# Linear attention and mixture of experts on one core: q and k loaded as whole runs, SyncE's queue in the order of the steps

## The chip, the cores and the metric

One core of a Trainium2 chip runs the whole program. The metric is the time of one execution on the device in microseconds. Engines are named as in the profile: PE is TensorE, PEld its weight loads, DVE is VectorE, ACT is ScalarE, POOL is GpSimd, SP is SyncE, whose queue issues nearly all transfers here (SPq in the rows).

## What is computed

Two parts follow each other. The first is attention with a feature map, on 8 batches of 8 heads with 576 tokens of 64 values; the second sends each token of the result (4608 rows of 512) through one of 8 experts, if its skip score is above 0.

```python
def phi(x):
    proj = np.einsum('bhsd,df->bhsf', x, w_phi)
    proj = proj - np.max(np.abs(proj), axis=-1, keepdims=True)
    return np.concatenate([np.exp(proj), np.exp(-proj)], axis=-1)
q_p, k_p = (phi(q), phi(k))
kv = np.einsum('bhsf,bhsd->bhfd', k_p, v)
z = np.sum(k_p, axis=2)
num = np.einsum('bhsf,bhfd->bhsd', q_p, kv)
den = np.einsum('bhsf,bhf->bhs', q_p, z)[..., None] + 1e-06
...
out = x.copy()
...
y[mask] = gate_w[mask, None] * (np.maximum(xc[mask] @ w1[e], 0.0) @ w2[e])
out[do_compute] = xc + y
```

## The kernel before

**Units and steps.** The attention works in units of four heads: 16 units of k and 16 of q, since a batch has two of each. A unit has five items. Item 0 is the tail, the last 2 tokens of each run of 18; items 1 to 4 are the other 16 tokens, in four parts. A head is 32 runs of 18 tokens, and a run is contiguous in memory. The program walks through steps: in step t, item t of the k stream and item t - 6 of the q stream enter, and each later stage takes the item that entered some steps earlier (projection 1, exponential 3, sums 4, use 5, and 6 for the table of a unit). So unit n of k enters in steps 5n to 5n+4, unit n of q in steps 5n+6 to 5n+10.

**A unit's way.** `st_load` (line 251) brings the unit into the tile `raw`. Its partitions are (half of d, head of the pair, run), and it holds 2 pairs of heads x 18 tokens x 32 values; one transfer per pair and half of d, so four per unit, in pieces of 32 values (128 bytes), because half of a token's 64 values lie together. `st_t` (line 276) transposes it on VectorE in 32 x 32 blocks: the tail at item 0 (line 289, tile `xTt`), and 512 columns each at items 1 and 3 (line 291, `xT`). ScalarE writes the rounded part `hi` (line 292), GpSimd or VectorE the rest `lo` (line 294), and TensorE projects both (lines 306 to 308). VectorE then takes the largest absolute value of each row (line 312) and subtracts it (line 321, tile `u`). For k, the exponentials are multiplied with `v` (lines 388 and 395); for q, with the table that comes of that (lines 465 and 486), and `norm` (lines 433 to 450) divides.

**Loads and stores.** `raw` has four buffers, `hi` and `lo` five each (pool `hl`). `f_t` asks for the next unit's load when a unit's item 0 enters, for either kind (line 720). `v` is asked for by `st_loadv` in step 5n+2 and its tails `vt` by `st_loadvt` in step 5n+3. Stores are put off by two steps (`store_half`, lines 503 and 505; `store_rows`, lines 564 and 566) and by seven (`rest`, lines 630 and 635); the stores of the attention's rows go to `xrows`, those of line 630 and 635 to the output.

**What sets the order.** Each engine runs its instructions in one fixed order, and SP its transfers too. A planner makes that order when the program is built: it takes what its own model says is ready, by the place in the program. TensorE is left out of that between steps 8 and 79, where its instructions stand in the program's order (`manual_schedule`, from line 724). SP's order is the planner's throughout. An instruction whose data has not come holds all behind it on its engine.

**The experts** follow: weights come in pieces of 512 KB (`load_chunk`, lines 184 and 187), ScalarE and VectorE or GpSimd split them into two parts (lines 188 and 189), TensorE multiplies, and rows are scattered to the output. Their tiles lie where the attention's were.

Of the kernel before, what the change touches and what calls it, by code (L numbers as in the profile page):

```python
# [8 lines left out]
F32 = mybir.dt.float32  # L9
# [9 lines left out]
P = 128  # L19
SLOT = 256  # L20
CFG = {'ql': -2, 'q1': 0, 'vtl': 3, 'at': 6, 'cp': 0, 'ini': 'vvpvppvvpvp', 'inz': '', 'lo': {('E', 0): 'pppvpppp', ('E', 1): 'pppppppp'}, 'lod': 'vppvvvpv', 'seq': ('E', 'E', 'C', 'C', 'SC', 'D', 'DS', 'C', 'C', 'D'), 'pre': (2,), 'rows': (1, 2), 'rxg': (0,) * 6, 'lag': (1, 3, 4, 5, 6), 'post': (4, 5, 7), 'hook': (-1, -1, -1), 'man': (8, 79), 'dnow': 0, 'off': 6, 'order': 'EPAZUT', 'direct': (), 'nb': {'K': 1, 'P': 3, 'U': 2, 'O': 2}, 'apools': (('ld', 2), ('hl', 5), ('up', 5), ('zp', 2), ('ep', 7), ('kvp', 6), ('xp', 2)), 'mpools': (('rawp', 1), ('mx', 2), ('mo', 2), ('wseta', 1), ('wsetb', 1))}
# [3 lines left out]
def kernel(  # L25
# [12 lines left out]
    nc = tc.nc  # L38
    B, H, S, D = q.shape
    NF = w_phi.shape[1]  # L40
    E = w_gate.shape[1]
# [9 lines left out]
    NAUG = D + E + 2  # L51
    NA1 = NAUG - 1
    # a row of xrows: the token, its gate, its number
# [3 lines left out]
    # slots: full ones, ones of up to 192 tokens, ones of up to 128  # L57
# [13 lines left out]
    xrows = dram.tile([NTOK, XW], F32, name="xrows")  # L71
# [35 lines left out]
    # the tails of a quad's v, each pair in its own rows, zeros in the other's  # L107
# [16 lines left out]
    # of every slot: the rows to gather and the rows to scatter to  # L124
# [85 lines left out]
    def places(g, pad, v):  # L210
        # v is 0 in an empty place, else 1 + the row to gather; what to add so that no row is scattered from an empty one
        nc.vector.tensor_scalar(out=g, in0=v, scalar1=-1.0, scalar2=0.0, op0=ALU.add, op1=ALU.max)
        nc.vector.tensor_scalar(out=pad, in0=v, scalar1=0.0, scalar2=BIG, op0=ALU.is_equal, op1=ALU.mult)

    early = []
    # ------------------------------------------------------------------ attention
    with ExitStack() as actx:
        pools = {}
        for nm, bufs in CFG["apools"]:
            pools[nm] = actx.enter_context(tc.tile_pool(name=nm, bufs=bufs))  # L220
        ld, hl, zp, up, ep, kvp, xp = (pools[nm] for nm in ("ld", "hl", "zp", "up", "ep", "kvp", "xp"))

        # a head is 32 runs of 18 tokens; partition (half of d, head of the pair, run)
        kv_in = {
            "k": k.rearrange("b h s d -> (b h s d)").rearrange("(u r p t c) -> u r p t c", r=2, p=64, t=18, c=D),
            "q": q.rearrange("b h s d -> (b h s d)").rearrange("(u r p t c) -> u r p t c", r=2, p=64, t=18, c=D),
        }
        vv = v.rearrange("b h s d -> (b h s d)").rearrange("(u h p t c) -> u p h t c", h=4, p=32, t=18, c=D)
        outv = out.rearrange("(b p j) m -> b p j m", p=32, j=18)
        # rows of xrows: two batches after each other, then the tails of both  # L230
# [20 lines left out]
        def st_load(u):  # L251
            src = kv_in[u.kind]
            u.raw = ld.tile([P, 2, 18, 32], F32, tag="raw", name="raw", bufs=4)
            for pr in range(2):
                for dh in range(2):
                    nc.sync.dma_start(
                        out=u.raw[dh * 64:dh * 64 + 64, pr],
                        in_=src[u.g, pr][:, :, dh * 32:dh * 32 + 32],
                    )
# [16 lines left out]
        def st_t(u, i):  # L276
            if i == 0:
                n, sfx = P, "t"
                src = u.raw[:, :, 16:18, :].rearrange("p r t c -> p r (t c)")
            elif i in (1, 3):  # L280
                n, sfx = 4 * P, ""
                src = u.raw[:, i // 2, 0:16, :].rearrange("p (q g) c -> p q g c", g=4)
            else:
                return
            xT = hl.tile([P, n], F32, tag="xT" + sfx, name="xT" + sfx, bufs=2)
            hi = hl.tile([P, n], F32R, tag="hi" + sfx, name="hi" + sfx)
            lo = hl.tile([P, n], F32R, tag="lo" + sfx, name="lo" + sfx)
            if i == 0:
                nc.vector.transpose(out=xT.rearrange("p (r c) -> p r c", r=2), in_=src)  # L289
            else:  # L290
                nc.vector.transpose(out=xT.rearrange("p (g q c) -> p q g c", g=4, q=4), in_=src)
            nc.scalar.activation(out=hi, in_=xT, func=AF.Copy)  # L292
# [140 lines left out]
        def norm(o, xdst, ldst, shape):  # L433
            # o: [P, 4, NAUG]
# [8 lines left out]
            a, c = shape  # L443
# [8 lines left out]
        def st_use_q(u, i):  # L452
# [5 lines left out]
            if i == 0:  # L458
                # the tails of two batches side by side
# [39 lines left out]
            if i == 4:  # L499
                c = slice(0, 4 * D)  # L500
# [12 lines left out]
        def post(b):  # L513
# [41 lines left out]
            # the gate goes with the token's row  # L555
# [21 lines left out]
            def rank():  # L577
                # rank of each computed token among those of its expert
# [133 lines left out]
        def f_t():  # L712
            for items, us, off in streams:
                s = now[0] - off
                if s == CFG["ql"]:
                    st_load(us[0])
                if 0 <= s < n:
                    u, i = items[s]
                    st_t(u, i)
                    if i == 0 and s // 5 + 1 < len(us):  # L720
                        st_load(us[s // 5 + 1])

        man = None
        for t in range(n + OFF + LA):
# [64 lines left out]
    def hidden_c(hv):  # L789
        # 192 tokens: the last 64 with both their parts next to each other  # L790
# [9 lines left out]
    def half1(ws, xs):  # L800
        # a slot of 128 tokens: the tokens' columns stay, the weights stream
# [53 lines left out]
    def mm1(ws, xs, hooks=()):  # L855
# [73 lines left out]
    # the slots of the tokens that are left: per expert full ones of 256, a rest of up to 192 or of up to 128 in  # L929
    # one of its own kind  # L930
# [5 lines left out]
    def tables():  # L936
# [24 lines left out]
        # a token's column: its rank, in groups of 128, plus cf[0] where it is below cf[1], else plus cf[2]  # L961
# [8 lines left out]
        # the experts of the slots, and how many there are  # L970
# [8 lines left out]
        # the column of each token  # L979
# [46 lines left out]
        # the slots that the sequence below leaves  # L1026
# [18 lines left out]
    # the slots in their order; a half one goes along with a full one  # L1045
# [50 lines left out]
    # whatever the slots above don't hold  # L1096
# [38 lines left out]
```

## Time and profile before

| | us |
|---|---|
| median of 3 runs | 684.47 |
| lowest and highest run | 684.28, 689.55 |
| span of the profiled execution, first to last instruction | 681.4 |
| attention runs evenly (stretch used below) | 20 to 350 |
| last attention work and tables of the experts | about 350 to 430 |
| experts | 430 to 681 |

The profile gives the span of one execution and no other time for it; the span is 3.1 us under the median of the runs. In its rows, a group is written as line, engine, operation, tile written <- tile read, shapes and count; then busy us, mean ns of one, and the idle time of the engine just before these instructions with what ended it. A timeline row starts with the start in us and the duration. A row of a stretch gives, for each engine, its busy time in it and the number of instructions.

### The profile page before, as it was taken

The numbers are of one execution on the slowest core, as the hardware profiler recorded it, in microseconds if no ns is written. First come the engines' busy times: TensorE is split into PE (matmuls) and PEld (weight loads), VectorE is DVE, ScalarE is ACT, GpSimd is POOL, SyncE is SP. The second block draws the span as 40 slices with busy tenths as digits, with TensorE's granted clock in tenths as the row PEclk, the third lists the DMA queues.
The fourth block names the chain that finished last, engine by engine and source line by source line (L and its number), as shares of the span: only waits on it lengthen the run. The fifth ranks groups of instructions, "written<-read, shape, count | busy, mean of one in ns | idle before, by whom it ended". The sixth has DMA issues, their size and how long they took to land. (4 is left out here: it accounts for less than half of the span.)

```text
span 681.4 us, 16258 instructions
## 1 busy us (share of the span) xinstructions
PE 600.5 (88%) x6045; PEld 514.2 (75%) x6045; DVE 539.6 (79%) x1216; ACT 373.7 (55%) x747; POOL 440.7 (65%) x383
## 2 busy tenths in 40 slices
PE   4897999979998889999899991999999989979994
PEld 3585888768877778877788881888878879868893
DVE  6868888887978978978998799679988876677830
ACT  4566665647565475656564533147757556555510
POOL 6886777777777596868774458276575485374411
PEclk9898999999999999999999996899989999999998
DMA  9898664857675667655316387269788877774500
GB/s 130 127 145 157 112 168 91 160 108 133 144 144 90 146 117 133 142 103 114 105 33 195 114 222 232 72 203 296 249 262 268 268 238 267 251 238 139 192 17 27
DMA packets 221684, 108.17 MB, mean 159 GB/s; under 512 B 160293, under 2 KB 202405, under 8 KB 221604
## 3 DMA queue, kind: packets, MB, share of 16 engines
q1 hardware_dynamic: 218272, 97.60, 58.8%
q0 software_dynamic: 3200, 9.45, 4.0%
q8 instruction: 49, 0.80, 0.5%
q14 instruction: 31, 0.25, 0.1%
q10 hardware_dynamic: 132, 0.07, 0.0%
HBM read 83.86 MB, written 24.02 MB: 158 GB/s over the span
## 5 line engine op out<-in xcount | busy, mean ns | idle before, releaser
L189 POOL TENSOR_TENSOR w<-wraw_c,w 128x1024 fp32r<-128x1024 f32 x45 | 109.9, 2454 | 70.6 <-ACT w L188 64.3
L188 ACT ACTIVATE w<-wraw_c 128x1024 fp32r<-128x1024 f32 x96 | 101.0, 1057 | 56.9 <-DMA wraw_c<-in_moe_w_dram 44.9
L353 POOL TENSOR_TENSOR z<-ek 128x512 f32<-128x512 f32 x64 | 81.7, 1277 | 54.9 <-ACT ek L345 45.1
L312 DVE TENSOR_REDUCE m<-ps_P 128x4 f32<-128x512 f32 (+1 forms) x160 | 96.4, 620 | 3.7 <-PE ps_P L308 3.6
L321 DVE TENSOR_TENSOR u<-ps_P,m 128x512 f32<-128x512 f32 (+1 forms) x160 | 95.9, 621 | 0.4
L306 PE MATMUL ps_P<-wph,hi 128*128 128x256 f32 x256 | 80.8, 316 | 16.6 <-ACT hi L292 8.5
L486 PEld LDWEIGHTS ps_O<-kva,eq 128*64 128x64 f32 x2048 | 75.2, 137 | 18.0 <-ACT eqt L373 7.3
L189 DVE TENSOR_TENSOR w<-wraw_c,w 128x1024 fp32r<-128x1024 f32 x51 | 75.4, 1481 | 14.6 <-ACT w L188 14.5
L486 PE MATMUL ps_O<-kva,eq 128*64 128x74 f32 x2048 | 78.4, 229 | 5.0 <-ACT eqt L373 3.2
L294 POOL TENSOR_TENSOR lo<-xT,hi 128x512 fp32r<-128x512 f32 x61 | 78.1, 1280 | 5.0 <-ACT hi L292 4.8
L308 PE MATMUL ps_P<-wph,lo 128*128 128x256 f32 x256 | 73.4, 287 | 0.0
L307 PE MATMUL ps_P<-wpl,hi 128*128 128x256 f32 x256 | 73.2, 286 | 0.0
L388 PE MATMUL ps_K<-ek,v 128*64 128x256 f32 x512 | 71.3, 396 | 1.5 <-DMA v<-in_v_dram 1.5
L372 ACT ACTIVATE eq<-ps_U 128x512 f32<-128x512 f32 x64 | 37.9, 593 | 57.2 <-PE ps_U L366 49.2
L306 PEld LDWEIGHTS ps_P<-wph,hi 128*128 128x128 f32 x256 | 49.4, 193 | 20.4 <-ACT hi L292 9.0
L908 PE MATMUL ps_O<-w,hh 128*128 128x512 f32 x160 | 62.4, 400 | 1.4 <-DVE hh L796 1.3
L836 POOL DMA_INDIRECT out_dram<-o,si x17 | 22.2, 1305 | 54.1 <-DVE o L834 44.4
L913 PE MATMUL ps_O<-w,hlo 128*128 128x512 f32 x120 | 49.0, 410 | 5.1 <-DVE hlo L796 5.1
L307 PEld LDWEIGHTS ps_P<-wpl,hi 128*128 128x128 f32 x256 | 49.7, 194 | 0.0
L308 PEld LDWEIGHTS ps_P<-wph,lo 128*128 128x128 f32 x256 | 49.6, 194 | 0.2 <-DVE lo L294 0.2
L366 PE MATMUL ps_U<-ident,u 128*128 128x128 f32 x288 | 48.4, 286 | 0.6 <-DVE u L321 0.6
L289 DVE STREAM_TRANSPOSE xTt<-raw 128x128 f32<-128x128 f32 x32 | 9.9, 309 | 48.8 <-DMA raw<-in_k_dram 26.8
(233 smaller groups left out, 1570.9 us busy)
## 6 DMA issues: line engine op xcount, KB each, us to landing
wraw_c<-in_moe_w_dram SPq DMA_DIRECT2D x96, 512.0 KB, 4.6
raw<-in_k_dram SPq DMA_DIRECT2D x64, 144.0 KB, 4.0
raw<-in_q_dram SPq DMA_DIRECT2D x64, 144.0 KB, 4.1
v<-in_v_dram SPq DMA_DIRECT2D x64, 128.0 KB, 3.7
out_dram<-xm SPq DMA_DIRECT2D x32, 256.0 KB, 4.4
xrows<-xm SPq DMA_DIRECT2D x8, 516.0 KB, 4.2
xrows<-xm SPq DMA_DIRECT2D x8, 512.0 KB, 4.7
vt<-in_v_dram SPq DMA_DIRECT2D x64, 16.0 KB, 2.6
```

The costliest lines, as they stand in the source:

```text
L188: nc.scalar.activation(out=hi, in_=raw, func=AF.Copy)
L189: (eng or nc.vector).tensor_tensor(out=lo, in0=raw, in1=hi.bitcast(F32), op=ALU.subtract)
L294: (nc.vector if CFG["ini"][nlo[0] - 1:nlo[0]] == "v" else nc.gpsimd).tensor_tensor(out=lo, in0=xT, in1=hi.bitcast(F32), op=ALU.subtract)
L306: nc.tensor.matmul(o, hi[:, c], wph, start=True, stop=False)
L307: nc.tensor.matmul(o, hi[:, c], wpl, start=False, stop=False)
L308: nc.tensor.matmul(o, lo[:, c], wph, start=False, stop=True)
L312: nc.vector.tensor_reduce(out=m[:, 0:nt], in_=pv, axis=AX.X, op=ALU.max, apply_absolute_value=True)
L321: nc.vector.tensor_tensor(out=uu[:, 0:nt, :], in0=pv, in1=m[:, 0:nt].rearrange("p (t o) -> p t o", o=1).broadcast_to([P, nt, NF]), op=ALU. ...
L353: zeng.tensor_tensor(out=z, in0=e[:, 0:2, :], in1=e[:, 2:4, :], op=ALU.add)
L388: nc.tensor.matmul(o[hd * 64:hd * 64 + 64, :], u.v[:, 2 * pr + hd, g * D:(g + 1) * D], u.e[i][:, 2 * j + hd, :], start=(g == 0), stop=False,)
L486: nc.tensor.matmul(ov[s * 64:s * 64 + 64, 2 * j + hd, :], e[:, half, j, hd, s * 64:s * 64 + 64], kva[:, half, 2 * pr + hd, :], start=(half ...
L908: nc.tensor.matmul(y[sub], hh[:, t], wh[:, fi, :], start=first, stop=False)
```

## The change

`raw` now holds all 64 values of each token: [128, 2, 18, 64], with three buffers. One transfer per half of d, so two per unit: each brings 64 partitions x 2 pairs, and for each the whole run of 18 tokens from the half's first value on, less the last 32 values, 1,120 values (4,480 bytes) in one piece. Both halves of d so arrive in either half of the partitions, and the transposes read the first 32 of every 64 values of a token. `hl` has four buffers for five. The next unit of q is asked for when item 3 of a q unit enters, and no longer item 0; for k it stays item 0. All that SP issues from the first step to the end of the attention is put in the program's order; the first unit's load stands before it and the experts' loads after it. Comments that the diff takes out are left out here.

```diff
-... ('hl', 5), ...
+... ('hl', 4), ...
...
-        kv_in = {
-            "k": k.rearrange("b h s d -> (b h s d)").rearrange("(u r p t c) -> u r p t c", r=2, p=64, t=18, c=D),
-            "q": q.rearrange("b h s d -> (b h s d)").rearrange("(u r p t c) -> u r p t c", r=2, p=64, t=18, c=D),
-        }
+        RUN = 18 * D
+        HD = D // 2
...
         def st_load(u):
-            src = kv_in[u.kind]
-            u.raw = ld.tile([P, 2, 18, 32], F32, tag="raw", name="raw", bufs=4)
-            for pr in range(2):
-                for dh in range(2):
-                    nc.sync.dma_start(
-                        out=u.raw[dh * 64:dh * 64 + 64, pr],
-                        in_=src[u.g, pr][:, :, dh * 32:dh * 32 + 32],
-                    )
+            x = q if u.kind == "q" else k
+            u.raw = ld.tile([P, 2, 18, D], F32, tag="raw", name="raw", bufs=3)
+            for r, run, n, dh in [(dh * 64, 0, 64, dh) for dh in range(2)]:
+                nc.sync.dma_start(
+                    out=u.raw[r:r + n].rearrange("p r t c -> p r (t c)")[:, :, 0:RUN - HD],
+                    in_=bass.AP(
+                        tensor=x.tensor, offset=x.offset + (u.g * 128 + run) * RUN + dh * HD,
+                        ap=[[RUN, n], [64 * RUN, 2], [1, RUN - HD]]))
...
-                src = u.raw[:, :, 16:18, :].rearrange("p r t c -> p r (t c)")
+                src = u.raw[:, :, 16:18, 0:HD]
...
-                src = u.raw[:, i // 2, 0:16, :].rearrange("p (q g) c -> p q g c", g=4)
+                src = u.raw[:, i // 2, 0:16, 0:HD].rearrange("p (q g) c -> p q g c", g=4)
...
-                nc.vector.transpose(out=xT.rearrange("p (r c) -> p r c", r=2), in_=src)
+                nc.vector.transpose(out=xT.rearrange("p (r t c) -> p r t c", r=2, t=2), in_=src)
...
-                    if i == 0 and s // 5 + 1 < len(us):
+                    if i == (0 if u.kind == "k" else 3) and s // 5 + 1 < len(us):
                         st_load(us[s // 5 + 1])
...
+        sman = actx.enter_context(ExitStack())
+        sman.enter_context(tc.manual_schedule(engines={mybir.EngineType.SP}))
         for t in range(n + OFF + LA):
...
             if t == 1:
                 setup()
+        sman.close()
```

More of the change, by code (lines that the diff above doesn't have):

```diff
@@ L20 @@
 SLOT = 256
-CFG = {'ql': -2, 'q1': 0, 'vtl': 3, 'at': 6, 'cp': 0, 'ini': 'vvpvppvvpvp', 'inz': '', 'lo': {('E', 0): 'pppvpppp', ('E', 1): 'pppppppp'}, 'lod': 'vppvvvpv', 'seq': ('E', 'E', 'C', 'C', 'SC', 'D', 'DS', 'C', 'C', 'D'), 'pre': (2,), 'rows': (1, 2), 'rxg': (0,) * 6, 'lag': (1, 3, 4, 5, 6), 'post': (4, 5, 7), 'hook': (-1, -1, -1), 'man': (8, 79), 'dnow': 0, 'off': 6, 'order': 'EPAZUT', 'direct': (), 'nb': {'K': 1, 'P': 3, 'U': 2, 'O': 2}, 'apools': (('ld', 2), ('hl', 5), ('up', 5), ('zp', 2), ('ep', 7), ('kvp', 6), ('xp', 2)), 'mpools': (('rawp', 1), ('mx', 2), ('mo', 2), ('wseta', 1), ('wsetb', 1))}
+CFG = {'ql': -2, 'q1': 0, 'vtl': 3, 'at': 6, 'cp': 0, 'ini': 'vvpvppvvpvp', 'inz': '', 'lo': {('E', 0): 'pppvpppp', ('E', 1): 'pppppppp'}, 'lod': 'vppvvvpv', 'seq': ('E', 'E', 'C', 'C', 'SC', 'D', 'DS', 'C', 'C', 'D'), 'pre': (2,), 'rows': (1, 2), 'rxg': (0,) * 6, 'lag': (1, 3, 4, 5, 6), 'post': (4, 5, 7), 'hook': (-1, -1, -1), 'man': (8, 79), 'dnow': 0, 'off': 6, 'order': 'EPAZUT', 'direct': (), 'nb': {'K': 1, 'P': 3, 'U': 2, 'O': 2}, 'apools': (('ld', 2), ('hl', 4), ('up', 5), ('zp', 2), ('ep', 7), ('kvp', 6), ('xp', 2)), 'mpools': (('rawp', 1), ('mx', 2), ('mo', 2), ('wseta', 1), ('wsetb', 1))}
 @with_exitstack
```

## The prediction

> **What bounds the kernel now.** I read the page's busy line first, then busy time by stretches, then who waits for whom, then single loads in the timeline.
>
> ```profile
> span 681.4 us, 16258 instructions
> PE 600.5 (88%) x6045; PEld 514.2 (75%) x6045; DVE 539.6 (79%) x1216; ACT 373.7 (55%) x747; POOL 440.7 (65%) x383
> ...
> 20.00:350.00 330.00, 301.17 (x3859) 251.48 (x3860) 275.74 (x765) 200.48 (x474) 251.64 (x240) 0.99 0.64 125
> ...
> L289 DVE STREAM_TRANSPOSE xTt<-raw 128x128 f32<-128x128 f32 x29 | 9.0, 310 | 48.2 <-DMA raw<-in_k_dram 26.2 <-DMA raw<-in_q_dram 18.2 <-POOL z L359 2.2
> L291 DVE STREAM_TRANSPOSE xT<-raw 128x512 f32<-128x512 f32 x59 | 41.2, 698 | 0.0
> L292 ACT ACTIVATE hi<-xT 128x512 fp32r<-128x512 f32 x58 | 36.4, 627 | 2.5 <-DVE xT L291 1.5 <-PE ps_P L307 0.6 <-DVE den L437 0.3
> ```
>
> The third line is the stretch in which the attention runs evenly. Columns: stretch, length, busy us of PE, PEld, DVE, ACT, POOL, then granted clock, DMA share, GB/s. By the whole span TensorE is the fullest engine. In this stretch VectorE is: 275.7 us busy and 48.2 us idle ahead of one instruction, the transpose of a unit's tail (line 289), make 323.9 of 330. TensorE leaves 330 - 301.2 = 28.8 us. So a microsecond more of waiting on `raw` costs about a microsecond, and one less gains at most until TensorE is full: 28.8 us in all. The 512-column transposes (line 291) never wait; the tail is the first reader of a unit and takes the whole wait.
>
> ```profile
> DVE xTt L289 <- DMA raw<-in_k_dram: 26.8, 14, 4.0
> DVE xTt L289 <- DMA raw<-in_q_dram: 18.2, 12, 3.4
> PE ps_P L306 <- DVE u L321: 12.3, 12, 3.8
> PE ps_O L486 <- ACT eqt L373: 3.2, 4, 1.1
> PE ps_O L486 <- DVE lgm L449: 1.4, 2, 0.8
> ACT w L188 <- DMA wraw_c<-in_moe_w_dram: 44.9, 39, 4.3
> ```
>
> Columns: us in total, times, longest. 45.0 us over 32 units is 1.41 us a unit. TensorE's answer to late VectorE work is 12.3 + 3.2 + 1.4 = 16.9 us.
>
> ```profile
> 163.04 3.10 SPq L256 DMA_DIRECT2D raw<-in_k_dram  x4
> 169.44 0.31 DVE L289 STREAM_TRANSPOSE xTt<-raw 128x128 f32<-128x128 f32 x1 [1.96 <-DMA raw<-in_k_dram]
> ...
> 289.26 2.21 SPq L256 DMA_DIRECT2D raw<-in_q_dram  x3
> 292.24 0.64 SPq L256 DMA_DIRECT2D raw<-in_q_dram  x1
> 298.10 0.31 DVE L289 STREAM_TRANSPOSE xTt<-raw 128x128 f32<-128x128 f32 x1 [3.44 <-DMA raw<-in_q_dram]
> 300.57 0.36 PE L306 MATMUL ps_P<-wph,hit 128*128 128x256 f32 x1 [1.47 <-DVE u L321]
> ```
>
> Two loads. The k load is first issued at 163.04; VectorE comes to its tail 4.44 us later (169.44 - 1.96 - 163.04) and the data 6.40 us later. The q load: 5.40 and 8.84. VectorE's order was fixed by the planner, which put the tail some 4.4 to 5.4 us of other work behind the load; the load takes 6.4 us or more. The wait is thus not late data as such, it is a tail queued too soon, and VectorE's other work stands behind it. The last row is TensorE paying 1.47 us of the 3.44.
>
> **The change part by part.**
>
> ```profile
> wraw_c<-in_moe_w_dram SPq DMA_DIRECT2D x96, 512.0 KB, 4.6
> raw<-in_k_dram SPq DMA_DIRECT2D x64, 144.0 KB, 4.0
> raw<-in_q_dram SPq DMA_DIRECT2D x64, 144.0 KB, 4.1
> v<-in_v_dram SPq DMA_DIRECT2D x64, 128.0 KB, 3.7
> ...
> 118.50:121.00 2.50, 2.50 (x33) 1.93 (x34) 2.43 (x8) 2.13 (x5) 0.74 (x1) 1.00 0.98 155
> 240.00:242.00 2.00, 1.67 (x22) 1.67 (x22) 0.60 (x4) 1.53 (x5) 2.00 (x3) 1.00 1.09 223
> 505.00:508.00 3.00, 3.00 (x25) 2.73 (x24) 3.00 (x5) 1.93 (x3) 1.73 (x1) 1.00 0.85 270
> ```
>
> The loads. A unit was 4 x 147,456 = 589,824 bytes in 128-byte pieces; the stretch at 118.5, where one such load runs, moved 155 GB/s with the DMA engines full (0.98): 589,824 / 155 = 3.8 us. Now each of two loads brings 64 partitions x 2 runs x 4,480 bytes = 573,440 bytes, both halves of d in either half of the partitions: 1,146,880 bytes a unit. The nearest rates for long pieces: v into 32 partitions, 223 GB/s at a full share (240 to 242), and weights into 128 partitions, 270 at 0.85, so 318 at a full one. That is 5.1 us or 3.6 us a unit. I take 223: a share of 1.09 says the engines were held up at that rate with 1-KB pieces, which a narrow destination explains, and 64 partitions are also not the whole width. The other end stays in the range.
>
> The Trainium skill, "SBUF — State Buffer", section "Door 1: The DMA port swizzle (why [64,N] ≈ [32,N])", says that partitions 0 to 63 reach only half of the DMA ports, so that 64 partitions get no more bandwidth than 32, and under "Can I just issue two DMAs to hit both halves?" that two such transfers serialize. By that rule the unit costs the 5.1 us and the sum below stands; without it 3.6 us, and the sum would be that of the third rival. The trace agrees as far as the 223 GB/s go; no run here yet shows 64 partitions with long runs.
>
> Time to land. v lands 3.7 us after issue, of which 131,072 bytes / 223 = 0.6 move: 3.1 us are fixed. A unit then lands 3.1 + 5.1 = 8.2 us after its first issue (3.1 + 3.6 = 6.7 at the fast rate), against 6.4 and 8.84 in the two rows above; four issues took 3.10 us of SP, two will take about half, which is inside the 8.2.
>
> Where VectorE stands then. Nothing shows where the planner will put the tails. Two ends: the distance stays at about 5 us, and the wait is 8.2 - 5 = 3.2 us, 1.8 more than 1.41, x 32 = +58 us; or the planner moves every tail behind its landing, and all 45.0 us go, of which TensorE lets 28.8 through. Between them I go by the row nearest in kind, the 96 weight loads of 512 KB in long pieces: ScalarE waits 44.9 / 96 = 0.47 us for one, so the planner's idea of such a load is short by that much at the fast rate. Two loads of that size at the slow rate are 5.1 - 3.6 = 1.5 us longer than at the fast one: 0.47 + 1.5 = 1.97 us a unit, 0.56 more than now, x 32 = +18 us. With VectorE full this is time of the kernel.
>
> Contention. 1.3 us more of transfer for each of the 29 units in 330 us brings the share from 0.64 to 0.64 + 38/330 = 0.75. DMA does not become the bound; loads that meet stores come later, which the upper end holds.
>
> ```profile
> SPq L503 <- DVE lgm L449: 15.1, 2, 9.3
> SPq L630 <- DVE lgm L449: 14.0, 3, 6.0
> SPq L564 <- DVE xt L561: 10.6, 3, 4.2
> SPq L635 <- DVE lgt L449: 8.3, 4, 3.5
> ```
>
> SyncE in the order of the steps. In a period of five steps SP now issues: k's next load (step 5n), the stores that fell due, v (5n+2), vt (5n+3), q's next load (moved from the q unit's item 0 to its item 3, step 5n+4). A store that waits for VectorE's norm holds v, vt and both loads behind it; these waits are already 15.1 + 14.0 + 10.6 + 8.3 = 48.0 us, in an order in which loads could pass. By the program q's load stands two steps ahead of its tail and k's five. The stretch holds 29 units, so a step is 330 / 29 / 2.5 = 4.6 us: 9.1 us for q against 8.2 to land, 23 for k. TensorE's need is met; what a held store costs appears as the tail's wait on VectorE. Price 0 to +48; I take 0, since the waits for q now (18.2), with v and vt partly ahead of it, are no larger than those for k (26.8).
>
> Three unit buffers. q n takes the buffer of k n, which is free at step 5n+3, one step before the load; k n+1 takes that of q n-2, free at 5n-1. No wait is added as long as VectorE keeps the program's order; price 0.
>
> `hl` from 5 to 4. ScalarE's write of `hi` waits for TensorE 0.6 us in all with five (the line 292 row above). With four a tile is asked for again five steps later and read for three; price 0 to a few times 0.6, I take 0.
>
> The strided transposes read 32 elements in 64. No row shows such a read; a penalty would lengthen the 698 ns, a gain isn't excluded by a row but has no cause. Taken as 0, the upper end in the range. One semaphore wait less or two per tail: nothing that I count.
>
> ```profile
> 7.11 0.71 DVE L291 STREAM_TRANSPOSE xT<-raw 128x512 f32<-128x512 f32 x1 [1.93 <-DMA raw<-in_k_dram]
> ...
> 0.79 8.87 SPq L256 DMA_DIRECT2D raw<-in_k_dram  x8
> ```
>
> The start. Now the first transpose needs the first two loads of four; then it needs both. 0.79 + 8.2 = 9.0 against 7.11: +2 us.
>
> ```profile
> 366.12 0.92 SPq L184 DMA_DIRECT2D wraw_c<-in_moe_w_dram  x1
> ...
> 397.37 0.57 SPq L566 DMA_DIRECT2D xrows<-xt  x1
> ```
>
> The end. The first expert weights are loaded at 366 among the attention's stores. They lie outside the ordered part, so they may still pass; were they held until the last store, 31 us later, TensorE would come to them cold. Price 0, else some of these 31.
>
> Sum: 18 + 2 = +20 on the profiled span of 681.4, so 701.4. The profile gives no time of its own beside its span; the runs' median of 684.47 is 3.1 above it, and I put the 3.1 around the new span too: 704.5.
>
> **The rivals.**
> 1. Faster: the tails fall behind their landings. Place: line 289. It decides where VectorE comes to the tail more than 8.2 - 1.41 = 6.8 us after the load's first issue. For it: k's load is asked for five steps ahead. Against it: the 4.44 and 5.40, tails pulled forward as soon as the planner thinks they can. TensorE's 16.9 us go, and the start costs 2: 684.5 - 15 = 669.5. If all its idle time went, 657.7.
> 2. No change: the planner counts the added bytes in full, and tail and landing move together. The start alone: 686.5.
> 3. The longer pieces pay in full: the loads run at the fast rate, land after 6.7 us and wait 0.47 us a unit. (1.41 - 0.47) x 32 = 30 us less, cut to the 16.9: 669.5 again.
> 4. Slower still: SP held by its stores. All 48 us shown: 704.5 + 48 = 752; half of it: 728.
>
> **How the numbers follow.** Forecast (704.5, its own range 692 to 730) and rival 4 together 0.45, of which rival 4 is 0.07; rival 2 0.18; rivals 1 and 3 0.29 and 0.08. A measurement of this kernel tells about 1% (6.8 us) from no change. Faster is 0.37, same 0.18, slower 0.45. Both signs hold much, so the range goes from 665 (most of the faster cases) to 728.
>
> **What would show it.** Right: line 289's idle time on `raw` above 48 us; two SP issues and 8 us to landing; a DMA share near 0.75 in the same stretch; 223 GB/s where a unit loads alone. Wrong: the share falls below 0.64 or the rate passes 300 GB/s (rate); the wait falls below 20 us and TensorE's share of the stretch rises above 0.95 (placing); SP idle on line 503 or 630 with a `raw` issue behind it (order).

## The result, and the profile after

The changed kernel takes 765.66 us (median of 4 runs, 761.41 to 766.63), the kernel before 684.38 us beside it (4 runs, 682.85 to 689.55). The ratio is 1.1146 with a 95% interval of 1.1093 to 1.1199: 81.3 us slower. The profiled execution has a span of 764.2 us.

First the page: span, busy time, and in 40 slices of the span VectorE's busy share and TensorE's granted clock, in tenths.

```profile
span 764.2 us, 16133 instructions
...
PE 629.9 (82%) x6045; PEld 535.9 (70%) x6045; DVE 531.2 (70%) x1216; ACT 375.5 (49%) x747; POOL 443.7 (58%) x383
...
DVE  2857676595596585676577887976887885567850
...
PEclk9879898898998898898899999969998999998998
```

The same 6045 matmuls are there, and no engine has notably more to do, but none is full any more. TensorE's busy time grew from 600.5 to 629.9 us with no instruction added; the mean clock granted to it was 0.917 in this execution and 0.974 in the one before the change. In the stretch that the prediction argued from, and in a short one with loads of q and k under way:

```profile
20.00:350.00 330.00, 270.81 (x3154) 223.37 (x3155) 226.57 (x622) 169.89 (x394) 210.64 (x200) 0.89 0.61 143
...
111.00:123.00 12.00, 5.96 (x101) 5.19 (x98) 5.94 (x22) 4.58 (x9) 5.62 (x9) 0.94 0.93 208
```

VectorE does 226.57 us of work in these 330 where it did 275.74, TensorE 3154 matmuls instead of 3859, at a clock of 0.89 instead of 0.99. The two transposes in the same stretch, as groups (busy us, mean ns, idle time ahead and what ended it), and who waits longest, on TensorE, over the span:

```profile
L289 DVE STREAM_TRANSPOSE xTt<-raw 128x128 f32<-128x128 f32 x25 | 7.8, 310 | 77.2 <-DMA raw<-in_q_dram 54.5 <-DMA raw<-in_k_dram 22.7
...
L291 DVE STREAM_TRANSPOSE xT<-raw 128x512 f32<-128x512 f32 x50 | 34.3, 689 | 1.0 <-POOL lo L294 1.0
...
PE ps_P L306 <- DVE u L321: 31.6, 10, 5.3
PE ps_O L406 <- DVE acc L625: 21.1, 5, 4.8
PE ps_P L306 <- ACT hi L292: 18.3, 1, 18.3
```

The wait is still at one place, the tail's transpose (line 289): 77.2 us for 25 tails, 3.1 us each, where it was 48.2 for 29. The 512-column ones behind it find their data there (their 1.0 us of waiting is for GpSimd's `lo`). The transposes are no slower: 310 and 689 ns against 310 and 698. TensorE's wait for VectorE's `u` went from 12.3 to 31.6 us.

SyncE's queue, by waits over the span, and one period of it beside VectorE in the timeline:

```profile
SPq L564 <- DVE xm L561: 80.7, 4, 24.6
SPq L564 <- DVE xt L561: 76.7, 3, 25.8
SPq L503 <- DVE lgm L449: 69.5, 8, 18.8
```

```profile
104.85 0.55 SPq L564 DMA_DIRECT2D xrows<-xm  x1
...
105.53 2.85 SPq L265 DMA_DIRECT2D v<-in_v_dram  x4
108.83 1.72 SPq L274 DMA_DIRECT2D vt<-in_v_dram  x4
110.59 1.27 SPq L255 DMA_DIRECT2D raw<-in_q_dram  x2
111.91 1.25 SPq L255 DMA_DIRECT2D raw<-in_k_dram  x2
113.21 2.02 SPq L630 DMA_DIRECT2D out_dram<-xm  x4
118.30 0.31 DVE L289 STREAM_TRANSPOSE xTt<-raw 128x128 f32<-128x128 f32 x1 [4.84 <-DMA raw<-in_q_dram]
...
124.00 0.31 DVE L289 STREAM_TRANSPOSE xTt<-raw 128x128 f32<-128x128 f32 x1 [1.77 <-DMA raw<-in_k_dram]
```

SP stands 226.9 us in these three rows and 230.9 at all the stores of lines 503 to 566; before, these made 41.9. The store at 104.85 is let go, and all that stood behind it goes in one burst: v, vt, q, k, within 8.3 us. The tail of q is reached 2.87 us after its load was issued (118.30 - 4.84 - 110.59) and its data comes after 7.7. The tail of k is reached 10.3 us after its own load was issued (124.00 - 1.77 - 111.91) and still waits: that load went out right behind q's, and its data comes after 12.1. (By the code, `v` is asked for in step 5n+1, in step 2 for the first unit; the stage `use` stands at four steps and the sums at five. SP's items follow each other in the same order.) From issue to landing of one load, by the page:

```profile
raw<-in_k_dram SPq DMA_DIRECT2D x32, 560.0 KB, 9.8
raw<-in_q_dram SPq DMA_DIRECT2D x32, 560.0 KB, 5.6
```

And the start, in the timeline; the last row is the kernel before:

```profile
10.17 0.71 DVE L291 STREAM_TRANSPOSE xT<-raw 128x512 f32<-128x512 f32 x1 [4.99 <-DMA raw<-in_k_dram]
...
17.05 0.69 ACT L95 ACTIVATE wph<-wsrc,own 128x128 fp32r<-128x128 f32 x2 [11.54 <-DMA wsrc<-in_w_phi_dram]
...
18.31 0.58 PE L306 MATMUL ps_P<-wph,hi 128*128 128x256 f32 x1 [18.31 <-ACT hi L292]
```

```profile
8.54 0.58 PE L306 MATMUL ps_P<-wph,hi 128*128 128x256 f32 x1 [8.54 <-ACT hi L292]
```

TensorE starts 9.8 us later. k's data is there at 10.17, 3.1 us later than the 7.11 before; what comes last, at 17, is w_phi, whose two loads ScalarE issues at the start.

### The profile page after: what moved, and what is told of

Its sections match the earlier page's. It is cut to its first block, busy times and chain, and to the rows that moved or that the text cites. A ratio compares the mean times of both kernels' runs of the same rounds, so it can differ in the third digit from the quotient of the medians.

```text
span 764.2 us, 16133 instructions
## 1 busy us (share of the span) xinstructions
PE 629.9 (82%) x6045; PEld 535.9 (70%) x6045; DVE 531.2 (70%) x1216; ACT 375.5 (49%) x747; POOL 443.7 (58%) x383
## 5 line engine op out<-in xcount | busy, mean ns | idle before, releaser
L306 PE MATMUL ps_P<-wph,hi 128*128 128x256 f32 x256 | 83.9, 328 | 47.8 <-DVE u L321 29.5
L486 PEld LDWEIGHTS ps_O<-kva,eq 128*64 128x64 f32 x2048 | 84.8, 152 | 18.3 <-ACT hi L292 6.6
L486 PE MATMUL ps_O<-kva,eq 128*64 128x74 f32 x2048 | 88.6, 246 | 1.6 <-ACT hi L292 0.9
L306 PEld LDWEIGHTS ps_P<-wph,hi 128*128 128x128 f32 x256 | 52.9, 207 | 51.2 <-issue 27.3
L189 DVE TENSOR_TENSOR w<-wraw_c,w 128x1024 fp32r<-128x1024 f32 x51 | 71.1, 1399 | 14.1 <-ACT w L188 14.0
L307 PE MATMUL ps_P<-wpl,hi 128*128 128x256 f32 x256 | 76.3, 298 | 0.0
L388 PE MATMUL ps_K<-ek,v 128*64 128x256 f32 x512 | 74.2, 408 | 0.1
L292 ACT ACTIVATE hit<-xTt 128x128 fp32r<-128x128 f32 x32 | 9.8, 308 | 101.4 <-DVE xTt L289 99.8
L307 PEld LDWEIGHTS ps_P<-wpl,hi 128*128 128x128 f32 x256 | 53.1, 208 | 0.0
L308 PEld LDWEIGHTS ps_P<-wph,lo 128*128 128x128 f32 x256 | 52.9, 207 | 0.1
```

What stands on the lines that cost most here:

```text
L189: (eng or nc.vector).tensor_tensor(out=lo, in0=raw, in1=hi.bitcast(F32), op=ALU.subtract)
L306: nc.tensor.matmul(o, hi[:, c], wph, start=True, stop=False)
L307: nc.tensor.matmul(o, hi[:, c], wpl, start=False, stop=False)
L308: nc.tensor.matmul(o, lo[:, c], wph, start=False, stop=True)
L388: nc.tensor.matmul(o[hd * 64:hd * 64 + 64, :], u.v[:, 2 * pr + hd, g * D:(g + 1) * D], u.e[i][:, 2 * j + hd, :], start=(g == 0), stop=False,)
L486: nc.tensor.matmul(ov[s * 64:s * 64 + 64, 2 * j + hd, :], e[:, half, j, hd, s * 64:s * 64 + 64], kva[:, half, 2 * pr + hd, :], start=(half ...
```

## The experiments

Each was timed beside the kernel before, which lay between 681.3 and 684.3 us in these comparisons. "Waits for raw" are VectorE's waits for q or k, summed over lines 289 and 291 of a run's table of waits. With every edit the planner makes its orders anew, so the order on other engines can differ too.

### One part alone: SyncE's order, and all but SyncE's order

`sp_order_only` is the kernel before with the lines that put SyncE's work in the program's order. `planner_order` is the changed kernel without them.

```diff
+        sman = actx.enter_context(ExitStack())
+        sman.enter_context(tc.manual_schedule(engines={mybir.EngineType.SP}))
...
+        sman.close()
```

> The kernel before with one part of the change alone: SyncE's loads and stores in the order of the steps. Short pieces, four loads per unit, four unit buffers and five of hl stay, and q's load stays at item 0. Theory 'order' (the stores hold the loads behind them, and that is the bulk of the 81 us): at least 725 us, SP idle on the store lines 503, 505, 564 and 566 rises from about 36 us to over 150. Theory 'bytes' (twice the bytes at half the rate are the bulk): 680 to 695 us. Theory 'tails' (what costs is how far the planner puts a unit's tail ahead of its data, whatever makes the data late): over 700 us if the wait on raw at line 289 passes 60 us, else near 684.

> The changed kernel with SyncE's order given back to the planner; the long runs, three unit buffers, four of hl and q's load at item 3 stay. Theory 'order': 685 to 700 us, and the waits on raw fall from 92.8 to about 50 us. Theory 'bytes': 740 us or more, waits on raw at 80 us or more, as the loads still take 8 us. Theory 'tails': between, about as far above 684 as the wait on raw is above 45 us, plus about 10 us of a later start.

732.04 us (ratio 1.0719, 1.0676 to 1.0762) and 738.00 us (1.0824, 1.0768 to 1.0881). Either part costs about 50 us without the other; together they cost 81, so part of the one is in the other. The next two runs say which. In `sp_order_only` SP stands 162.1 us at the stores, as the theory 'order' said. The theory 'tails' failed there: line 289 waits only 45.1 us for raw, and 31.6 more are at line 291, the 512-column transposes.

### The long runs undone, and the buffers alone

`bufs3_only` is the kernel before with three buffers of `raw`, four of `hl`, and q's load at item 3. `short_runs` adds SyncE's order to that; it is the changed kernel with 128-byte pieces again.

```diff
-            u.raw = ld.tile([P, 2, 18, 32], F32, tag="raw", name="raw", bufs=4)
+            u.raw = ld.tile([P, 2, 18, 32], F32, tag="raw", name="raw", bufs=3)
...
-                    if i == 0 and s // 5 + 1 < len(us):
+                    if i == (0 if u.kind == "k" else 3) and s // 5 + 1 < len(us):
```

> The kernel before with three buffers of raw instead of four, four of hi and lo instead of five, and q's next load at item 3; loads stay in 128-byte pieces, SyncE in the planner's order. Theory (of the part of the change that is not SyncE's order, the slow long runs cost, not the buffers): within 1% of the kernel before, 678 to 691 us, raw_k and raw_q waits of VectorE together 40 to 55 us. Rival (fewer buffers and the later load of q cost it): 715 to 740, the whole of what after_planner_order lost, with waits for raw of 65 us or more.

> The changed kernel with its loads in 128-byte pieces again: SyncE's order, three buffers, q's next load at item 3. Theory (the order and the long runs are the two causes): 725 to 740 us, like sp_order_only (732.0). Rival 1 (buffers and the later load of q share in the loss): 745 to 766. Rival 2 (q's load at item 3 helps under SyncE's order, since it no longer stands ahead of the held store): under 720.

684.64 us (1.0044, 1.0003 to 1.0084) and 712.08 (1.0441, 1.0372 to 1.0510). With the buffers as in the changed kernel, the account closes:

| us (waits for raw) | planner's order | order of the steps |
|---|---|---|
| 128-byte pieces | 684.6 (29.3) | 712.1 (55.8) |
| long runs | 738.0 (79.4) | 765.7 (97.8) |

The order costs 27.5 or 27.7 us, the long runs (with the strided transposes that go with them) 53.4 or 53.6, whichever stands beside them. The four runs come from different comparisons; as differences from the kernel before beside each, the long runs cost 51.5 or 51.6, the order the same as above. The waits for raw rise by 26.5 for the order and 50.1 for the long runs, nearly the time lost; for both together they rise by 68.5 against 81.1. The wait counts need not go one to one with time: between the kernel before (47.7) and `bufs3_only` (29.3) they differ and the time doesn't. By rival 2 of `short_runs`, the order costs less with q's load at item 3 (712.1) than at item 0 with four buffers (732.0). These two runs differ in the number of buffers too, which was not tried apart.

Where the waits come from is seen in the timeline of `planner_order`:

```profile
122.06 1.26 SPq L255 DMA_DIRECT2D raw<-in_q_dram  x2
123.43 1.25 SPq L255 DMA_DIRECT2D raw<-in_k_dram  x2
...
130.09 0.31 DVE L289 STREAM_TRANSPOSE xTt<-raw 128x128 f32<-128x128 f32 x1 [3.92 <-DMA raw<-in_q_dram]
...
135.65 0.31 DVE L289 STREAM_TRANSPOSE xTt<-raw 128x128 f32<-128x128 f32 x1 [2.52 <-DMA raw<-in_k_dram]
```

The tail of q is reached 4.1 us after its load's first issue, and the data comes after 8.0. k's load goes out 1.4 us behind q's: its tail is reached after 9.7 us, and its data comes after 12.2. From 60 to 352 us all eleven units of each kind go this way: q is reached after 4.1 to 6.5 us and lands after 7.8 to 9.3, a wait of 3.2 us in the mean; k, issued 1.4 to 4.3 us behind q, is reached after 7.3 to 10.1 and lands after 9.7 to 12.8, a wait of 2.4.

### The tails held back

VectorE's order was changed in one place: the tail's transpose may not be placed ahead of the subtraction (line 321) of the step two before.

```diff
-            nc.vector.tensor_tensor(
+            last_u[now[0]] = nc.vector.tensor_tensor(
                 out=uu[:, 0:nt, :], in0=pv,
...
-                nc.vector.transpose(out=xT..., in_=src)
+                with (tc.issue_after(last_u[now[0] - 2].ins) if now[0] - 2 in last_u else ExitStack()):
+                    nc.vector.transpose(out=xT..., in_=src)
```

> The kernel before with the same restraint on the tails. Theory 'tails': the waits on raw fall from 45.0 to under 15 us and the time to 665 to 675 us, which would beat both kernels. If late data is what counts, or TensorE takes the gain, 680 to 686 us.

> The changed kernel with VectorE's order touched alone: a unit's tail may not stand ahead of the subtraction (line 321) of two steps before its own step. Loads, buffers and SyncE's order stay. Theory 'tails': the data comes in time for its step and only the queue is wrong, so the waits on raw fall from 92.8 to under 30 us and the time to about 700 us, of which some 10 us are the start. Theories 'order' and 'bytes' (the data itself is late): the waits stay above 70 us and the time above 745 us.

> The long runs in the planner's order, with the tails' transposes not placed ahead of the subtraction of two steps before (the restraint that took the kernel before from 684.3 to 664.6). Theory (of the 54 us of the long runs, 10 are the start, where w_phi stands behind k's first packets; the rest are transposes that stand in VectorE's queue for data that lands 8 to 10 us after its issue instead of 4): 690 to 715. Rival (with half the rate the data itself is late, so the wait moves on to the 512-column transposes): 720 to 738, with L291's waits for raw above 40 us.

664.62 us (0.9748, 0.9693 to 0.9802), 742.14 (1.0869, 1.0822 to 1.0915) and 685.50 (1.0045, 1.0016 to 1.0075). The stretch from 60 to 350 us, in `before_tails2` and in `long_tails2`:

```profile
60.00:350.00 290.00, 276.58 (x3647) 232.09 (x3642) 255.41 (x727) 182.57 (x428) 228.04 (x217) 0.99 0.62 127
```

```profile
60.00:350.00 290.00, 273.95 (x3604) 230.18 (x3598) 248.42 (x701) 180.05 (x428) 224.73 (x215) 0.99 0.70 174
```

In the planner's order the restraint takes 738.0 to 685.5 and the waits for raw from 79.4 to 7.1, and from 60 us on TensorE is nearly as full with the slow loads beside it as without (0.99 clock, 3604 matmuls against 3647). There the data was early enough for TensorE; it was late for a transpose that had been put ahead of other work of VectorE. The kernel before had 20 us of the same loss. So with the restraint in both, the long runs (and the buffers) still cost 20.9 us, 685.5 against 664.6, of the 53. Of these, 9.7 are there at TensorE's first matmul (18.27 us against 8.53) and 11.4 at its first one of line 486 (51.2 against 39.8): they belong to the start. `long_tails2` with nothing but w_phi's load put first was not run.

In the order of the steps the restraint finds less, and the table of waits of `after_tails2` says why:

```profile
DVE xT L291 <- DMA raw<-in_q_dram: 61.8, 14, 6.5
DVE xT L291 <- DMA raw<-in_k_dram: 4.6, 1, 4.6
```

The wait went on to the 512-column transposes, which the restraint does not hold: here q's data is issued late.

### The stores off SyncE's queue

`sp_stores_later` and `after_stores_later` issue the stores five steps after their item in place of two. `sp_stores_act` and `after_stores_act` have ScalarE issue them, whose order is the planner's.

```diff
-                    later.append((now[0] + 2, store_half))
+                    later.append((now[0] + 5, store_half))
...
-                later.append((now[0] + 2, store_rows))
+                later.append((now[0] + 5, store_rows))
```

```diff
-                        nc.sync.dma_start(out=rowm[b][:, :, c], in_=xm[:, :, c])
+                        nc.scalar.dma_start(out=rowm[b][:, :, c], in_=xm[:, :, c])
```

(the second diff at all four stores, lines 503 to 566)

> sp_order_only with the stores of xm, xt issued five steps after the item that makes them instead of two, so that their data is there when SyncE comes to them. Theory (the order costs because SyncE stands at a store and the loads queue up behind it): SyncE's waits at lines 503, 564 and 566 fall from 158 us to under 50, VectorE's waits for raw from 75 to under 50, the time from 732.0 to 675 to 705. Rival (loads come late in that order for another cause, as being issued at the step that the order names instead of ahead of it): 720 to 735.

> The changed kernel with the same later stores. Theory (held stores cost what SyncE's order added to the long runs, 765.7 less 738.0): 725 to 742 us, SyncE's waits at lines 503, 564, 566 under 60 instead of 227. Rival (the long runs themselves, issued in a burst, make the data late): 750 to 766, with waits for raw above 80.

> sp_order_only (732.0) with the stores of xm and xt issued by ScalarE instead of SyncE. Moving them five steps later (sp_stores_later, 726.0) only moved SyncE's stand from line 564 to 503 (112.3 us), so this takes them off its queue. Theory (loads are late because SyncE stands at a store ahead of them): 675 to 700 us, and VectorE's waits for raw fall from 75 us to 50 or less. Rival (the order itself makes the loads late, or ScalarE now stands at the stores): 715 to 740.

> The changed kernel with the stores of xm and xt issued by ScalarE. Theory (held stores are what SyncE's order adds to the long runs, 28 of the 81 us): 735 to 745, as after_planner_order (738.0). Rival 1 (they are more than that; with the loads issued early the long runs are hidden too): under 725. Rival 2 (the burst is late for another reason): 750 to 766.

Put off, 726.01 us (1.0623, 1.0541 to 1.0706) and 750.62 (1.0954, 1.0878 to 1.1029). From ScalarE, 701.85 (1.0267, 1.0196 to 1.0339) and 741.35 (1.0857, 1.0801 to 1.0913). SP's longest wait in `sp_stores_later`, then in `sp_stores_act`:

```profile
SPq L503 <- DVE lgm L449: 112.3, 7, 20.9
```

```profile
SPq L265 <- PE ps_K L388: 110.8, 12, 12.6
```

Putting the stores off was a poor test: it freed line 564, and the store at line 503 then waited instead, by the code for later writes to the same tile `xm`. Both times came out in the range of the rival, though in `after_stores_later` the waits for raw fell from 97.8 to 58.0 us, against what that rival said. Off the queue, they give back 30.2 of the order's 47.7 us without the long runs, and 24.3 of its 27.7 with them: 741.35 is the 738.00 of `planner_order` within the runs. So with the long runs the held stores are what the order cost. Without them 17.5 us remain (701.85, just above the theory's 700), though the waits for raw, 41.2 us, are no more than the 47.7 of the kernel before; they are gone only with the tails held back as well (`sp_fix` below). SP then stands at the load of v instead (line 265), which waits for TensorE to free one of its two buffers.

### The start

`after_wsrc` has SyncE load w_phi ahead of the first k. `after_wsrc4` leaves it to ScalarE, in four loads of 32 rows in place of two with an outer dimension of two.

```diff
-            nc.scalar.dma_start(
-                out=wsrc[dh * 64:dh * 64 + 64],
-                in_=bass.AP(tensor=w_phi.tensor, offset=w_phi.offset + dh * 32 * NF, ap=[[0, 2], [NF, 32], [1, NF]]))
+            for hd in range(2):
+                nc.scalar.dma_start(
+                    out=wsrc[dh * 64 + hd * 32:dh * 64 + hd * 32 + 32], in_=w_phi[dh * 32:dh * 32 + 32])
```

> The changed kernel with w_phi's two loads issued by SyncE ahead of the first load of k instead of by ScalarE beside it. Theory (the start lost 9.8 us because w_phi's packets stood behind long ones on the DMA engines): TensorE's first matmul at 9 to 11 us instead of 18.3, the time 755 to 759 instead of 765.7. Rival (the first units wait for k0 and v0 anyway): the first matmul is earlier, the time stays within 3 us of 765.7.

> The changed kernel with w_phi loaded by ScalarE in four loads of 32 rows instead of two whose outer dimension of two repeats the rows. Theory (two engines alone carry each of the two loads, behind their share of k's long packets): ScalarE's wait for w_phi falls from 11.5 us to 3 to 6, TensorE's first matmul from 18.3 to 11 to 13 us, the time to 757 to 762, as after_wsrc (760.7). Rival (the place behind k's packets alone is what counts): the wait stays above 9 us, the time within 3 us of 765.7.

760.66 us (758.60 to 765.04) and 767.58 (761.53 to 768.28). Of `after_wsrc4`:

```profile
12.43 0.58 PE L306 MATMUL ps_P<-wph,hi 128*128 128x256 f32 x1 [12.43 <-ACT wph L95]
```

In `after_wsrc` the first matmul is at 11.91, later than the theory's 9 to 11, and then waits for `hi`, made of k's data. The reason was right, the price not. In four loads w_phi comes early enough to start TensorE at 12.43 instead of 18.31, issued from the same place beside k's; and nothing of the 5.9 us is left at the end. Its waits for raw are 107.3 against 97.8: a unit that is reached earlier waits longer for its load. The 5.0 us of `after_wsrc` lie in runs that overlap those of the changed kernel.

### The rate of the long loads

`after_pr` and `long_fix_pr` cut a unit's loads by pair of heads, so that each writes all 128 partitions, with the same packets and bytes (`long_fix_pr`: in the planner's order, tails held back, w_phi first). `long_actq` is `long_tails2` with the second load of a unit issued by ScalarE.

```diff
-            for r, run, n, dh in [(dh * 64, 0, 64, dh) for dh in range(2)]:
+            for pr in range(2):
                 nc.sync.dma_start(
...
-                        ap=[[RUN, n], [64 * RUN, 2], [1, RUN - HD]]))
+                        ap=[[HD, 2], [RUN, 64], [1, RUN - HD]]))
```

> The changed kernel with a unit's two loads cut by pair of heads instead of by half of d: each writes all 128 partitions, one packet of 4480 bytes to each, the same bytes and packets as before. Theory (the half rate comes from one load reaching 64 partitions only, so that the two loads of a unit follow each other at half rate): a load's landing falls from 9.8 (k) and 5.6 us (q) to 4 to 6, packets of 4480 bytes take about half as long, the time falls from 765.7 to 715 to 745. Rival (the rate is bound by the doubled bytes or by the packet itself): landing and time as before, 758 to 770.

> long_tails2 with w_phi first and the loads cut by pair: long runs in the planner's order without the start's loss and at the full rate if there is one. Theory (the 21 us by which long_tails2 is over before_tails2 are the start and the slow loads): 662 to 672. Rival (doubled bytes cost by themselves): 676 to 686.

> long_tails2 (685.5) with the second of a unit's two loads issued by ScalarE, so that the loads of both halves of the partitions can be under way together. Theory (sixteen engines writing 64 partitions share half of the way into the memory): a unit's landing falls from 8.2 (k) and 7.3 us (q) to 4.5 to 6, the rate in a burst rises from about 210 to above 260 GB/s, the time to 672 to 682. Rival (the rate is bound by the reading, or by the engines, whichever partitions are written): landing 7 us or more, rate as before, time 683 to 692 or worse, as ScalarE now stands at the loads.

1282.93 us (1.8809, 1.8699 to 1.8918), 1199.68 (1.7593, 1.7479 to 1.7708) and 689.72 (1.0111, 1.0077 to 1.0146): three misses. `after_pr` in the stretch from 111 to 123 us, where it does little but load:

```profile
111.00:123.00 12.00, 0.24 (x1) 0.24 (x2) 2.22 (x5) 1.34 (x4) 0.46 (x1) 0.50 0.13 53
```

A DMA share of 0.13 is two of the sixteen engines (2/16 = 0.125). The source's outer dimension is now the two halves of d, and the load goes to two engines. So the runs did not test what they were made for, but they gave another number: 53 / (16 x 0.13) = 25 GB/s for one engine, against 208 / (16 x 0.93) = 14 in the same stretch of the changed kernel, with the same packets. Each of the sixteen engines that write 64 partitions gets 0.55 of what each of the two does. The two runs differ in the number of engines at work as well as in the partitions that a load reaches. In `long_actq` both halves are under way at once, and a load's median landing, by the page:

```profile
raw<-in_k_dram SPq DMA_DIRECT2D x16, 560.0 KB, 8.0
raw<-in_k_dram ACTq DMA_DIRECT2D x16, 560.0 KB, 11.0
raw<-in_q_dram SPq DMA_DIRECT2D x16, 560.0 KB, 5.6
raw<-in_q_dram ACTq DMA_DIRECT2D x16, 560.0 KB, 8.0
```

In `long_tails2` the medians over both loads of a unit are 8.2 us (k) and 7.3 (q). Here the first load lands after 8.0 and 5.6 us, the second after 11.0 and 8.0, where 4.5 to 6 was expected: two queues don't bring a higher rate here.

### All remedies together

`after_all` is the changed kernel with stores from ScalarE, tails held back and w_phi first; `sp_fix` the kernel before with SyncE's order, stores from ScalarE and tails held back.

> The changed kernel with all three remedies: stores of xm and xt from ScalarE, tails' transposes not ahead of the subtraction of two steps before, w_phi loaded first by SyncE. Theory (these three are the whole loss): 675 to 690, that is long_tails2 (685.5) less some of the start's 5. Rival (SyncE's order has a cost of its own, as the loads of v that stand for their buffer ahead of q and k): 695 to 725.

> The kernel before with SyncE in the order of the steps, the stores from ScalarE, and the restraint on the tails' transposes. Theory (SyncE's order costs only through held loads and transposes that stand for them): 662 to 672, like before_tails2 (664.6). Rival (loads of v hold SyncE, 110.8 us at line 265 in sp_stores_act, and make q and k late also without the early transposes): 680 to 700.

688.98 us (1.0109, 1.0040 to 1.0179) and 661.26 us (0.9675, 0.9612 to 0.9737). The three remedies take back 76.7 of the 81.3 us, with all parts of the change in place. But the first two help the kernel before too: `sp_fix` is 20.7 us faster than the kernel before beside it. So with the remedies on both sides the change still costs 27.7 us (688.98 against 661.26); 8.1 of these are there at TensorE's first matmul of line 486 (48.6 against 40.5 us), and where the others arise was not followed. The even stretch of `sp_fix`:

```profile
60.00:350.00 290.00, 282.93 (x3754) 237.19 (x3750) 261.97 (x749) 187.22 (x440) 230.73 (x219) 1.00 0.65 133
```

TensorE is busy 0.98 of the stretch at full clock. From `before_tails2` (664.62) it isn't told apart, as the intervals overlap: SyncE's order by itself, once nothing is held in it and nothing is placed too early behind it, neither costs nor clearly gains.

## Why the prediction was wrong

The direction was its likeliest case, the size was four times too small: +20 forecast, +81 measured, outside the range. Two terms of the sum failed, and of the 61 us that it lacks about 28 are SyncE's order and 33 the long runs.

**SyncE in the order of the steps: taken as 0, measured 27.5 to 47.7** (27.7 beside the other parts of the change). This step failed outright: a cost that came was put at nothing. The mechanism was named (a held store holds v, vt and both loads) and bounded from 0 to +48, and then set to 0, because "the waits for q now (18.2) ... are no larger than those for k (26.8)". That row came from an order in which the planner had put each store about where its data is ready. It cannot tell how long SP stands when it runs ahead to a store in the program's order: 230.9 us in place of 41.9. The lead of 9.1 us for q counted steps of the program, while a load's lead begins when the store ahead is let go: 2.87 us in the row shown. `after_stores_act` and `sp_stores_act` show the cause: without the stores in the queue 24 of the 28 us are gone, and 30 of the 48 without the long runs.

**The wait at the tail: +18 taken (+20 with the start), +53 measured for the long runs, start and all.** The mechanism was right, a term was mis-sized. The ends were +58 (the tail keeps its distance behind the load) and a gain (the planner moves it behind the landing). In `planner_order` q's tails kept their distance (4.1 to 6.5 us) and their landing was the 8.2 foretold (7.8 to 9.3), so they wait 3.2 us, as at that end. k's tails did move, to 7.3 to 10.1 us; but the landing of 8.2 was that of a unit by itself, and k's load goes out behind q's and lands after 9.7 to 12.8. Over 32 units the waits for raw are 79.4 us, 2.5 a unit against the 1.97 taken; and they rose from the 29.3 us that the changed buffers leave (`bufs3_only`), not from the 45.0 of the sum. The middle of 1.97 came from ScalarE's waits for the experts' weights, another engine's work in another stage, which did not carry over. `long_tails2` shows what the first rival would have needed, and nothing placed the tails so.

**The range** joined neither upper end to the other. 58 for the tails and 48 for the order were both on paper; the fourth rival, with all 48, gave 752 at a chance of 0.07, and the range stopped at 728, its half.

**The rate was right.** 223 GB/s were taken; 208 at a share of 0.93 are 224 at a full one. The page "SBUF — State Buffer" of the Trainium skill, section "Door 1: The DMA port swizzle (why [64,N] ≈ [32,N])", says that partitions 0 to 63 and 64 to 127 reach half of the ports each, and "Can I just issue two DMAs to hit both halves?" that two loads, one to each half, serialize. The 14 against 25 GB/s an engine fits the one and `long_actq` the other. That the narrow destination is the cause is not shown: a load of all 128 partitions on sixteen engines, with these long runs, was not tried.

**What bounds the kernel.** That a microsecond of waiting on `raw` costs about a microsecond held for each part alone (26.5 for 27.5, 50.1 for 53.4). For both together 12.6 us are left over (81.1 less 68.5). TensorE's lower clock lies beside it; whether it is the cause stays open. Nor does it hold downwards: in `after_stores_later` the waits fell by 39.8 us and the time by 15.0. And part of the long runs' 53.4 is the start, where TensorE waits for w_phi and not for `raw`, so that the closeness of 50.1 to 53.4 is in part luck.

**Three buffers, `hl`, strided transposes: 0 each.** Right within what the runs tell: 684.64 us for the buffers with the later load, 2.2 above the kernel before beside it, and 689 and 310 ns for the transposes against 698 and 310.

**Contention** was taken to bring the share from 0.64 to 0.75. It is 0.61, since the stretch does less work; with the waits gone it is 0.70 (`long_tails2`, from 60 to 350).

**The start**: +2 taken, 9.8 measured at the first matmul; the first transpose, for which the +2 was meant, came 3.1 us later (10.17 against 7.11). w_phi's load was overlooked. Putting it right alone gained little or nothing at the end of the changed kernel's run.

**The end**: taken as 0. The experts' first weights are loaded at 454.23, the last store to `xrows` goes at 477.40, so loads still pass:

```profile
454.23 3.54 SPq L184 DMA_DIRECT2D wraw_c<-in_moe_w_dram  x4
...
477.40 0.56 SPq L566 DMA_DIRECT2D xrows<-xt  x1
```

## What to carry to other kernels

A queue in program order runs ahead to the first instruction whose data isn't made yet and stands there: before you fix such an order, take stores out of the queue of the loads, or place each store where its data exists. When a wait for a load looks like late data, look at how long after the load's issue the waiting engine comes to it; holding back the one instruction that was placed too early was worth 20 us to the kernel before and 52 with the slow loads in the planner's order. Try such a remedy on the kernel before as well, or its worth is counted as a cost of the change. When two loads go out back to back, price the landing of the second behind the first. And where two costs have both been bounded, the range has to hold the sum of their upper ends, not one of them.

## What was not expected of the hardware

- An access pattern whose outer dimension is two keeps a load on two of the sixteen DMA engines: a share of 0.13 and 53 GB/s in `after_pr`, and 1283 us in place of 766. The Trainium skill states this in "DMA: Bandwidth & Descriptors", section "Rules for kernel authors" (an outermost dimension below 16 confines the whole transfer to at most that many engines); the trace agrees. w_phi's two loads have such a dimension too: issued at 0.78 and 2.02 us beside k's long packets, they kept ScalarE waiting until 17.05, while four loads without it, from the same place, landed 6.2 us after issue (median, by the page of `after_wsrc4`). How many engines carried w_phi was not read.
- TensorE was granted a lower clock in the runs in which it stood more. The mean granted clock was 0.974 before, 0.917 after and 0.762 in `after_pr`, with TensorE busy for 88, 82 and 52% of the span, and the same 6045 matmuls took 600.5, 629.9 and 666.9 us of busy time. No run changes the gaps alone, so that they lower the clock is not shown, and in short stretches it need not follow: after the change it was 0.94 from 111 to 123 us, with TensorE busy for half of that time, and 0.89 from 20 to 350, with 82%.
